# One DFF tile per weight piece: reordering how float64 weights are loaded and split in an attention and two-MLP kernel

## The chip, the cores and the metric

The kernel runs on one core of one Trainium2 chip. The metric is the device time of one execution in microseconds, the median over several runs. Engines are called as the profile calls them: PE (TensorE matmuls) and PEld (its weight loads), DVE (VectorE), ACT (ScalarE), POOL (GpSimd) and SP (SyncE, which here only issues DMAs).

## The reference

A causal attention (4 batches, 8 heads, 576 positions, head size 64; half the heads see a local window of 32, the others every 32nd position) is followed by two MLPs over 2304 tokens, each `512 -> 2048 -> 512`:

```python
scores = np.where(masks[None], scale * np.matmul(q, k.transpose(0, 1, 3, 2)), -1e9)
attn = np.exp(scores - np.max(scores, axis=-1, keepdims=True))
attn = attn / (np.sum(attn, axis=-1, keepdims=True) + 1e-09)
x = np.matmul(attn, v)            # to (2304, 512)
h = np.maximum(x @ w_in, 0.0)     # w_in  512 x 2048, float64
x = (h * h) @ w_out               # w_out 2048 x 512, float64; twice, with other weights
```

## The kernel before

**Numbers in two parts.** A matmul operand is held as a rounded part (`hi`, float32r) and a remainder (`lo`). Each product of the MLPs is three matmuls: hi by hi, hi by lo, lo by hi. The weights arrive as float64 words and are taken apart on chip, piece by piece. A piece is 128 partitions by 512 float64 (512 KB), and there are 32 in each layer. Four functions, each one step of a piece's way, are laid out in the list `conv` so that consecutive entries belong to four consecutive pieces: `sign_and_end` (two DVE instructions, L212 and L215), `exponent_range` (ACT, L221), `together` (DVE, L226), `in_parts` (ACT writes hi, L239; DVE writes lo, L240). Call the DVE part of them S, T and P. `conv_by(1)` emits the next entry of the list, wherever the program stands.

**Pieces before.** Groups of eight: four "in" pieces, each holding 128 of the 512 rows of `w_in` for 1024 words (four DFF tiles of 128 columns), then four "out" pieces, each 128 rows of `w_out`.

**Steps.** The MLP runs in 144 steps `s`, one for each token block and DFF tile: 16 steps a block of 512 tokens (8 steps, with two tiles each, for a block of 256), five blocks a layer. Layer 1 is steps 0 to 71, layer 2 steps 72 to 143. `mm1(s)` makes 12 matmuls into `ps_h` (L677); then ACT applies the ReLU (`r`, L689) and squares it into `gh` (L692), DVE squares again into `sq` (L693) and subtracts to get the remainder `gl` (L694). `mm2(s)` makes 12 matmuls into `ps_y` (L728). The program, and so each engine's queue, goes `mm1(s+1)`, `mm2(s)`, `mm1(s+2)`, `mm2(s+1)`. Each step has eight places called `point()`: three inside `mm1`, one behind it (behind r, gh, sq, gl), three inside `mm2`, one behind it. At a point, entries of the attention lists are emitted, and then one `conv` entry while the layer's pieces last.

**Attention.** Twelve fills of the first batch run alone ahead of the MLP, in the rounds of `ALONE`. After each round `START_LOAD` tells how many pieces are loaded and `START_CONV` how many conv entries are emitted. The fills of the second batch (`SHARED`) run at the points of steps 0 to 15, those of the others later. One fill has on PE scores (L417), transposes (L460), values (L476) and a last transpose (L522), on DVE a mask with maximum (L437, four pairs), a division (L507, L508, L510) and a remainder (L564).

**Between the layers.** At the end of the steps with `f % 4 == 3` of layer 1's last block (steps 59, 63, 67, 71), eight pieces of layer 2 are loaded into the slots that the old pieces leave; conv entries run at every point from step 62 on.

**Order.** No scheduler reorders anything: each engine runs its instructions in the order in which the program emits them, and all loads go through SP's queue.

Of the kernel before, what the change touches and what calls it, by code (L numbers as in the profile page):

```python
# [12 lines left out]
AF = mybir.ActivationFunctionType  # L13
ALU = mybir.AluOpType
AX = mybir.AxisListType

P = 128
# [5 lines left out]
KC = DM // P  # L23
NF = DFF // P
# [6 lines left out]
NB = len(BLOCKS[0])  # L31
# [10 lines left out]

N_PT = 8

START_LOAD = (0, 0, 0, 1, 2, 2, 4, 2, 2, 4, 2, 5, 4, 2, 2)
START_CONV = (3, 0, 0, 0, 0, 0, 0, 4, 8, 4, 2, 1, 3, 3, 6)
GAP = 80

FIRST_2 = 2
# [88 lines left out]
def r32(ap):  # L138
    return ap.bitcast(F32)
# [3 lines left out]
def tile_attention_then_two_mlps(  # L143
# [9 lines left out]
    nc = tc.nc  # L153
# [19 lines left out]
    wt = {}  # L173
    pieces = []
    for layer in range(2):
        for g in range(4):
            pieces += [("in", layer, g, c) for c in range(KC)]
            pieces += [("out", layer, g, c) for c in range(4)]
    half1 = len(pieces) // 2
    n_load = [0]  # L180
    raw, val = {}, {}

    def load_piece():

        n = n_load[0]
        if n >= len(pieces):
            return
        kind, layer, g, c = pieces[n]
        raw[n] = wpool.tile([P, 512, 2], I32, tag=f"w{n % half1}", name="raw")
        n_load[0] += 1  # L190
        if kind == "in":
            src = w_in[layer][c * P:(c + 1) * P, g * 1024:(g + 1) * 1024]
        else:
            src = w_out[layer][(4 * g + c) * P:(4 * g + c + 1) * P, :]
        nc.sync.dma_start(out=raw[n].rearrange("p n w -> p (n w)"), in_=src)

    def load_ahead(n):

# [49 lines left out]
    n_conv, n_part = [0], [0]  # L248

    def conv_by(n):  # L250

        while n and n_conv[0] < len(conv):
            fn, i = conv[n_conv[0]]
            if i >= n_load[0]:
                return
            fn(i)
            n_conv[0] += 1
            n -= 1
            n_part[0] += fn is in_parts

    def ready(key):
        while key not in wt:
            conv_by(1)
        return wt[key]
# [105 lines left out]
    def load_v():  # L370
        i = n_vin[0]
        if i >= NFILL:
            return
        n_vin[0] += 1
        _, v = src_of(i)
        vin[i] = fpool.tile([P, VW], F32, tag="v", name="v", bufs=5)
        nc.sync.dma_start(out=vin[i][:, :v.shape[-1]], in_=v)
# [115 lines left out]
    def one_small():  # L493
        if small:
            small.pop(0)()
# [130 lines left out]
    blocks = [(layer, j) for layer in range(2) for j in range(NB)]  # L626

    def tiles_of(k):
        layer, j = blocks[k]
        return TB // BLOCKS[layer][j][1]  # L630
# [23 lines left out]
    def block_x(k):  # L654
        layer, j = blocks[k]
        return (xh[j], xl[j]) if layer == 0 else xin[k]

    def mm1(s, point):

        if s >= len(steps):  # L660
            return
        k, f = steps[s]
        ne = tiles_of(k)
        n = TB // ne
        x_hi, x_lo = block_x(k)
        g, f0 = divmod(f, 4)
        if n_att[0] < len(att):
            ps = ps_h.tile([P, TB], F32, tag="h", name="ps_h")
        else:
            ps = ps_a.tile([P, TB], F32, tag="a", name="ps_h")  # L670
        for c in range(KC):
            w = ready(("in", blocks[k][0], g, c))
            for e in range(ne):
                cols = slice((f0 + e) * P, (f0 + e + 1) * P)
                for i, (a, x) in enumerate(((0, x_hi), (0, x_lo), (1, x_hi))):

                    nc.tensor.matmul(  # L677
                        ps[:, e * n:(e + 1) * n],
                        lhsT=w[:, a, cols],
                        rhs=x[:, c, :n],  # L680
                        start=c == 0 and e == 0 and i == 0,
                        stop=c == KC - 1 and i == 2 and e == ne - 1,
                    )
                    one_small()
            if c < KC - 1:
                point()
        r = gpool.tile([P, TB], F32, tag="r", name="r", bufs=1)
        sq = gpool.tile([P, TB], F32, tag="sq", name="sq", bufs=1)
        nc.scalar.activation(out=r, in_=ps, func=AF.Relu, scale=W_BACK)  # L689
        h = gpool.tile([P, TB], F32R, tag="gh", name="gh", bufs=2)  # L690
        lo = gpool.tile([P, TB], F32R, tag="gl", name="gl", bufs=2)
        nc.scalar.activation(out=h, in_=r, func=AF.Square)  # L692
        nc.vector.tensor_tensor(out=sq, in0=r, in1=r, op=ALU.mult)  # L693
        nc.vector.tensor_tensor(out=lo, in0=sq, in1=r32(h), op=ALU.subtract)  # L694
        gh[s], gl[s] = h, lo

    def mm2(s, point):
        k, f = steps[s]
        layer, j = blocks[k]
        t0, n = BLOCKS[layer][j]  # L700
        ne = tiles_of(k)
        g, f0 = divmod(f, 4)
        ws = [ready(("out", layer, g, f0 + e)) for e in range(ne)]
        h, lo = gh.pop(s), gl.pop(s)

        ny = KC if layer == 0 else n // P
        if f == 0:
            ys[k] = [ps_y.tile([P, 512], F32, tag=f"y{c}", name="ps_y") for c in range(ny)]
        end = f + ne == NF
        todo = []  # L710
        for c, y in enumerate(ys[k]):
            cols = slice(c * P, (c + 1) * P)
            for i, (a, gp) in enumerate(((0, h), (1, h), (0, lo))):
                for e, w in enumerate(ws):
                    g0 = e * n
                    rows = slice(g0 + c * P, g0 + (c + 1) * P)
                    if layer == 1:
                        todo.append((i, c, y, gp[:, rows], w[:, a]))
                    else:
                        todo.append((i, c, y[:, :n], w[:, a, cols], gp[:, g0:g0 + n]))  # L720
        if not end:

            todo.sort(key=lambda t: t[0] == 2)
        places = [-(-len(todo) * (i + 1) // 4) - 1 for i in range(3)]
        last = {t[1]: m for m, t in enumerate(todo)}
        seen = set()
        for m, (i, c, y, lhsT, rhs) in enumerate(todo):
            nc.tensor.matmul(  # L728
                y, lhsT=lhsT, rhs=rhs, start=f == 0 and c not in seen, stop=end and m == last[c]
            )  # L730
            seen.add(c)
            one_small()
            if end and m == last[c]:
                t = apool.tile([P, 512], F32, tag="pt", name="o")
                if layer == 0:
                    t = t[:, :n]
                nc.scalar.activation(out=t, in_=y, func=AF.Copy, scale=W_BACK)  # L737
                if layer == 0:
                    nc.sync.dma_start(out=y_dram[:, c, t0:t0 + n], in_=t)
                else:  # L740
                    nc.sync.dma_start(out=out[t0 + c * P:t0 + (c + 1) * P, :], in_=t)
            if m in places:
                point()
# [13 lines left out]
    with tc.manual_schedule():  # L757
        nc.scalar.dma_start(out=cst, in_=consts)
        for n in range(5):
            if n < 3:  # L760
                load_qk()
            load_v()
        rounds = 0
        while n_att[0] < att_end[0]:
            att_to(min(n_att[0] + len(ALONE), att_end[0]))
            load_ahead(START_LOAD[rounds])
            conv_by(START_CONV[rounds])
            rounds += 1
        def nothing():
            pass  # L770

        mm1(0, nothing)
        for s in range(len(steps)):
            k, f = steps[s]
            layer, j = blocks[k]
            n_pt = [0]
            load_ahead(4)
            for fn, k2, c in y_at.get(s, ()):
                fn(k2, c)

            def point(s=s, layer=layer, j=j, f=f):
                n_pt[0] += 1
                at = N_PT * s + n_pt[0]
                for b, (p0, p1) in enumerate(spans):
                    if at > p0:
                        lo, hi = att_end[b], att_end[b + 1]
                        att_to(min(hi, lo + -(-(hi - lo) * (at - p0) // (p1 - p0))))
                if n_part[0] < half1 or layer == 1 or j == NB - 1 and f > 5:
                    conv_by(1)

            mm1(s + 1, point)
            point()
            mm2(s, point)
            point()
            if layer == 0 and j == NB - 1 and f % 4 == 3:
                for _ in range(8):
                    load_piece()

# [35 lines left out]
```

## Time and profile before

| | |
|---|---|
| median of 3 runs | 923.03 us (920.58 to 923.31) |
| profiled execution, its own time | 921.91 us |
| its span | 920.1 us |
| PE / PEld busy | 898.3 / 754.5 us |
| DVE / ACT busy | 483.0 / 389.6 us |
| HBM read / written | 61.67 / 9.44 MB |

The span is what the profiler saw of the program from its first to its last instruction; the execution's own time is 1.8 us longer. Busy time of PE counts a matmul from its start to a modelled end, so that matmuls overlap.

### The profile page before, as it was taken

The numbers are of one execution on the slowest core, as the hardware profiler recorded it, in microseconds if no ns is written. First come the engines' busy times: TensorE is split into PE (matmuls) and PEld (weight loads), VectorE is DVE, ScalarE is ACT, GpSimd is POOL, SyncE is SP. The second block draws the span as 40 slices with busy tenths as digits, with TensorE's granted clock in tenths as the row PEclk, the third lists the DMA queues.
The fourth block names the chain that finished last, engine by engine and source line by source line (L and its number), as shares of the span: only waits on it lengthen the run. The fifth ranks groups of instructions, "written<-read, shape, count | busy, mean of one in ns | idle before, by whom it ended". The sixth has DMA issues, their size and how long they took to land.

```text
span 920.1 us, 12461 instructions
## 1 busy us (share of the span) xinstructions
PE 898.3 (98%) x4624; PEld 754.5 (82%) x4624; DVE 483.0 (52%) x1234; ACT 389.6 (42%) x825; POOL 0.2 (0%) x4
## 2 busy tenths in 40 slices
PE   7799999999999999999999999999999999999998
PEld 6778888877788888899887677888888888888897
DVE  5999995576666665222289996222322233222221
ACT  5656773555555544322256664232223232322222
POOL 0000000000000000000000000000000000000000
PEclk9599999999999999999999999999999999999999
DMA  8856520222222110100555140010001000100010
GB/s 271 287 171 218 191 89 13 84 79 69 87 68 101 54 61 12 46 1 24 206 194 194 61 191 12 12 69 1 23 1 69 1 24 0 58 6 7 1 46 24
DMA packets 31597, 71.92 MB, mean 78 GB/s; under 512 B 3504, under 2 KB 11824, under 8 KB 31536
## 3 DMA queue, kind: packets, MB, share of 16 engines
q1 hardware_dynamic: 31392, 70.86, 22.5%
q8 instruction: 37, 0.61, 0.3%
q10 hardware_dynamic: 144, 0.26, 0.1%
q14 instruction: 24, 0.20, 0.1%
HBM read 61.67 MB, written 9.44 MB: 77 GB/s over the span
## 4 chain that ended last, share of the span: by engine, by line
PE 86%; DVE 9%; DMA 2%; ACT 2%; issue 1%; DVEq 0%; ACTq 0%
PE ps_h L677 39%; PE ps_y L728 38%; PE ps_o L476 3%; PE ps_s L417 2%; DVE val L226 2%; DMA qk<-st_qk_d 2%; DVE w L240 2%; DVE raw L215 2%; PE ps_pt L460 2%; DVE gl L694 1%; PE ps_s L323 1%; ACT raw L221 1%; DVE raw L212 1%; PE ps_x L522 1%; ACT r L689 1%
## 5 line engine op out<-in xcount | busy, mean ns | idle before, releaser
L677 PE MATMUL ps_h<-xh,w 128*128 128x512 f32 (+1 forms) x1280 | 404.3, 376 | 4.4 <-ACT r L689 4.4
L693 DVE TENSOR_TENSOR sq<-r 128x512 f32<-128x512 f32 x144 | 99.5, 691 | 360.3 <-ACT r L689 360.0
L677 PEld LDWEIGHTS ps_h<-xh,w 128*128 128x128 f32 x1280 | 234.4, 190 | 46.8 <-ACT r L689 8.2
L689 ACT ACTIVATE r<-ps_h 128x512 f32<-128x512 f32 x144 | 86.0, 597 | 379.5 <-PE ps_h L677 349.7
L677 PE MATMUL ps_h<-xl,w 128*128 128x512 f32 (+1 forms) x640 | 237.4, 371 | 0.0
L728 PE MATMUL ps_y<-gh,w 128*128 128x512 f32 (+1 forms) x640 | 155.6, 375 | 0.0
L728 PE MATMUL ps_y<-w,gh 128*128 128x512 f32 x576 | 145.0, 390 | 0.0
L677 PEld LDWEIGHTS ps_h<-xl,w 128*128 128x128 f32 x640 | 121.4, 190 | 16.7
L728 PEld LDWEIGHTS ps_y<-w,gh 128*128 128x128 f32 x576 | 107.5, 188 | 22.6 <-ACT o L737 0.7
L728 PEld LDWEIGHTS ps_y<-gh,w 128*128 128x128 f32 x640 | 108.2, 189 | 16.7
L694 DVE TENSOR_TENSOR gl<-sq,gh 128x512 fp32r<-128x512 f32 x144 | 99.7, 693 | 17.9
L692 ACT ACTIVATE gh<-r 128x512 fp32r<-128x512 f32 x144 | 91.2, 633 | 4.6
L728 PE MATMUL ps_y<-gl,w 128*128 128x512 f32 (+1 forms) x320 | 85.2, 375 | 0.8 <-DVE gl L694 0.8
L728 PE MATMUL ps_y<-w,gl 128*128 128x512 f32 x288 | 79.1, 389 | 0.0
L728 PEld LDWEIGHTS ps_y<-gl,w 128*128 128x128 f32 x320 | 55.0, 189 | 10.7 <-DVE gl L694 1.9
L728 PEld LDWEIGHTS ps_y<-w,gl 128*128 128x128 f32 x288 | 54.1, 188 | 11.2
L453 ACT ACTIVATE s<-s,m 96x128 f32<-96x128 f32 (+2 forms) x176 | 55.9, 389 | 4.9 <-DVE m L437 4.3
L221 ACT ACTIVATE raw<-raw 128x512 f32<-128x512 f32 x64 | 43.0, 675 | 20.3 <-DVE raw L215 20.0
L239 ACT ACTIVATE w<-val 128x512 fp32r<-128x512 f32 x64 | 40.2, 629 | 22.5 <-DVE val L226 22.5
L476 PEld LDWEIGHTS ps_o<-v,pt 128*96 128x96 f32 (+2 forms) x352 | 45.2, 183 | 5.0
L215 DVE SCALAR_TENSOR_TENSOR raw<-raw 128x512 int32<-128x512 int32 x64 | 44.4, 694 | 2.2
L476 PE MATMUL ps_o<-v,pt 128*96 128x65 f32 (+2 forms) x352 | 44.4, 261 | 0.0
(34 smaller groups left out, 543.3 us busy)
## 6 DMA issues: line engine op xcount, KB each, us to landing
raw<-moe_w_in_d SPq DMA_DIRECT2D x32, 512.0 KB, 5.3
raw<-moe_w_out_d SPq DMA_DIRECT2D x32, 512.0 KB, 7.1
qk<-loc_qk_d SPq DMA_DIRECT2D x12, 416.0 KB, 3.1
out_d<-o SPq DMA_DIRECT2D x18, 256.0 KB, 2.0
y_dram<-o SPq DMA_DIRECT2D x16, 256.0 KB, 2.0
y_in<-y_dram SPq DMA_DIRECT2D x16, 256.0 KB, 2.9
qk<-loc_qk_d SPq DMA_DIRECT2D x12, 304.0 KB, 3.4
v<-loc_v_d SPq DMA_DIRECT2D x24, 130.0 KB, 2.9
```

Of the source, the lines that this page charges most:

```text
L215: nc.vector.scalar_tensor_tensor(out=lower, in0=upper, scalar=-(2 ** 31), in1=lower, op0=ALU.bitwise_and, op1=ALU.bitwise_or)
L221: nc.scalar.activation(out=upper, in_=upper, func=AF.Copy, scale=2.0 ** (W_EXP // 8 - 112))
L226: nc.vector.scalar_tensor_tensor(out=val[n].bitcast(I32), in0=upper, scalar=3, in1=lower, op0=ALU.logical_shift_left, op1=ALU.bitwise_or,)
L239: nc.scalar.activation(out=w[:, 0], in_=v, func=AF.Copy)
L453: nc.scalar.activation(out=blk, in_=blk, func=AF.Exp, scale=-1.0, bias=m[:nq, j:j + 1])
L476: nc.tensor.matmul(ps[:nq, j * W:(j + 1) * W], lhsT=pt[:nk, j * nq:(j + 1) * nq], rhs=t[:nk, j * W:(j + 1) * W], start=True, stop=True,)
L677: nc.tensor.matmul(ps[:, e * n:(e + 1) * n], lhsT=w[:, a, cols], rhs=x[:, c, :n], start=c == 0 and e == 0 and i == 0, stop=c == KC - 1 and ...
L689: nc.scalar.activation(out=r, in_=ps, func=AF.Relu, scale=W_BACK)
L692: nc.scalar.activation(out=h, in_=r, func=AF.Square)
L693: nc.vector.tensor_tensor(out=sq, in0=r, in1=r, op=ALU.mult)
L694: nc.vector.tensor_tensor(out=lo, in0=sq, in1=r32(h), op=ALU.subtract)
L728: nc.tensor.matmul(y, lhsT=lhsT, rhs=rhs, start=f == 0 and c not in seen, stop=end and m == last[c])
```

## The change

A piece of `w_in` holds all 512 rows for one DFF tile, as four runs of 1 KB in each partition where it had one run of 4 KB. Pieces alternate: "in" of tile 0, "out" of tile 0, "in" of tile 1, and so on; a step of a 512-token block needs one of each. The tables for the time of the first batch are new: 31 conv entries before, 19 now; loads are later too. Between the layers two pieces are loaded at the end of each step of the last block (56 to 71), and conv entries run from step 59 at three of four points. While loaded pieces wait to be taken apart, ACT makes `sq` (Square) and then `gh` (Copy of `sq`), and DVE only `gl`. In code:

```diff
-START_LOAD = (0, 0, 0, 1, 2, 2, 4, 2, 2, 4, 2, 5, 4, 2, 2)
-START_CONV = (3, 0, 0, 0, 0, 0, 0, 4, 8, 4, 2, 1, 3, 3, 6)
+START_LOAD = (0, 0, 0, 1, 0, 1, 0, 1, 0, 1, 1, 1, 1, 2, 2)
+START_CONV = (0, 0, 0, 0, 0, 0, 0, 0, 0, 2, 3, 3, 3, 4, 4)
...
-        for g in range(4):
-            pieces += [("in", layer, g, c) for c in range(KC)]
-            pieces += [("out", layer, g, c) for c in range(4)]
+        for f in range(NF):
+            pieces += [("in", layer, f), ("out", layer, f)]
...
+            dst = dst.rearrange("p (c m) -> p c m", c=KC)
+            src = w_in[layer].rearrange("(c p) m -> p c m", p=P)[:, :, 2 * f * P:2 * (f + 1) * P]
...
         for c in range(KC):
-            w = ready(("in", blocks[k][0], g, c))
             for e in range(ne):
+                w = ready(("in", blocks[k][0], f + e))
...
-        nc.scalar.activation(out=h, in_=r, func=AF.Square)
-        nc.vector.tensor_tensor(out=sq, in0=r, in1=r, op=ALU.mult)
+        if 0 < n_load[0] - n_part[0]:
+
+            nc.scalar.activation(out=sq, in_=r, func=AF.Square)
+            nc.scalar.activation(out=h, in_=sq, func=AF.Copy)
+        else:
+            nc.scalar.activation(out=h, in_=r, func=AF.Square)
+            nc.vector.tensor_tensor(out=sq, in0=r, in1=r, op=ALU.mult)
...
-                if n_part[0] < half1 or layer == 1 or j == NB - 1 and f > 5:
+                if n_part[0] < half1 or (layer == 1 or j == NB - 1 and f > 2) and n_pt[0] % 4:
                     conv_by(1)
...
-            if layer == 0 and j == NB - 1 and f % 4 == 3:
-                for _ in range(8):
+            if layer == 0 and j == NB - 1:
+                for _ in range(2):
                     load_piece()
```

PE's order is the same in both kernels but for which weights a matmul reads. The order in the queues is shown at two places; names carry buffer numbers where these tell pieces apart.

Place one, step 4 of layer 1. DVE before, around the remainder `gl_1009` of `mm1(4)`; `w_1033` is an "out" piece that PE first reads in `mm2(5)`:

```order
L693 TENSOR_TENSOR sq_1006<-r_1005 128x512
L694 TENSOR_TENSOR gl_1009<-sq_1006,gh_1008 128x512
L212 TENSOR_SCALAR raw_870<-raw_870 128x512
L215 SCALAR_TENSOR_TENSOR raw_870<-raw_870 128x512
L226 SCALAR_TENSOR_TENSOR val_1027<-raw_781 128x512
L240 TENSOR_TENSOR w_1033<-val_983,w_1033 128x512
L564 TENSOR_TENSOR xl_304<-ps_x_1024,xh_303 128x192
```

DVE of the change at the same place, around `gl_979` of `mm1(4)`; `w_1003` is the "in" piece of tile 5:

```order
L241 TENSOR_TENSOR w_969<-val_903,w_969 128x512
L698 TENSOR_TENSOR gl_979<-sq_976,gh_978 128x512
L213 TENSOR_SCALAR raw_840<-raw_840 128x512
L216 SCALAR_TENSOR_TENSOR raw_840<-raw_840 128x512
L227 SCALAR_TENSOR_TENSOR val_997<-raw_751 128x512
L241 TENSOR_TENSOR w_1003<-val_953,w_1003 128x512
L565 TENSOR_TENSOR xl_300<-ps_x_994,xh_299 128x192
```

The square has left DVE; S, T and P behind `gl` stand as before, but the P there now makes the weights of the next `mm1`. PE of the change from the last matmul of `mm1(4)` (`ps_h_927`) over the second half of `mm2(3)` to the start of `mm1(5)` (`ps_h_1021`), with what a matmul waits for:

```order
L676 MATMUL ps_h_927<-xh_212,w_909 128x512
L731 MATMUL ps_y_726<-gh_884,w_875 128x512 x2
L731 MATMUL ps_y_723<-gl_885,w_875 128x512
L731 MATMUL ps_y_724<-gl_885,w_875 128x512
L731 MATMUL ps_y_725<-gl_885,w_875 128x512
L731 MATMUL ps_y_726<-gl_885,w_875 128x512
L676 MATMUL ps_h_1021<-xh_212,w_1003 128x512 [waits Activation_49]
L477 MATMUL ps_o_1014<-v_553,pt_988 96x65 [waits DMAHW3_49,DVE_49]
L676 MATMUL ps_h_1021<-xl_213,w_1003 128x512
L477 MATMUL ps_o_1014<-v_553,pt_988 96x65
L676 MATMUL ps_h_1021<-xh_212,w_1003 128x512 [waits DVE_49]
```

The third matmul of `mm1(5)`, the first that reads the lo part of `w_1003`, now has a wait for DVE; in the kernel before, `mm1(5)` has none.

Place two, between the layers. DVE before, from one `gl` to the next (steps 67 and 68):

```order
L694 TENSOR_TENSOR gl<-sq,gh 128x512
L226 SCALAR_TENSOR_TENSOR val<-raw 128x512
L240 TENSOR_TENSOR w<-val,w 128x512
L212 TENSOR_SCALAR raw<-raw 128x512
L215 SCALAR_TENSOR_TENSOR raw<-raw 128x512
L650 TENSOR_TENSOR xl_4860<-y_in,xh_4859 128x512
L226 SCALAR_TENSOR_TENSOR val<-raw 128x512
L240 TENSOR_TENSOR w<-val,w 128x512
L212 TENSOR_SCALAR raw<-raw 128x512
L215 SCALAR_TENSOR_TENSOR raw<-raw 128x512
L693 TENSOR_TENSOR sq<-r 128x512
L694 TENSOR_TENSOR gl<-sq,gh 128x512
```

DVE of the change at the same steps:

```order
L698 TENSOR_TENSOR gl<-sq,gh 128x512
L241 TENSOR_TENSOR w<-val,w 128x512
L213 TENSOR_SCALAR raw<-raw 128x512
L216 SCALAR_TENSOR_TENSOR raw<-raw 128x512
L651 TENSOR_TENSOR xl_4870<-y_in,xh_4869 128x512
L227 SCALAR_TENSOR_TENSOR val<-raw 128x512
L241 TENSOR_TENSOR w<-val,w 128x512
L213 TENSOR_SCALAR raw<-raw 128x512
L216 SCALAR_TENSOR_TENSOR raw<-raw 128x512
L698 TENSOR_TENSOR gl<-sq,gh 128x512
```

One T and the square are gone from this step; other steps lose more, since six conv entries, not eight, stand in a step.

## Rows read from the trace of the kernel before

**Rows 1.** Windows: us; busy PE, PEld, DVE, ACT, POOL; PEclk, DMA share, GB/s.

```profile
22.00:45.00 23.00, 17.30 (x91) 15.63 (x91) 20.81 (x77) 15.46 (x45) 0.00 (x0) 0.57 0.86 297
55.00:156.00 101.00, 101.00 (x571) 84.74 (x570) 90.35 (x255) 65.13 (x153) 0.00 (x0) 1.00 0.41 135
482.00:568.00 86.00, 81.48 (x345) 63.46 (x344) 80.78 (x140) 52.59 (x90) 0.00 (x0) 1.00 0.33 123
568.00:920.00 352.00, 348.50 (x1628) 292.12 (x1626) 96.21 (x143) 94.49 (x160) 0.00 (x0) 1.00 0.07 22
```

**Rows 2.** Waits of PE, 0 to 46 us: total, times, longest.

```profile
PE ps_s L417 <- DMA qk<-st_qk_d: 4.5, 3, 2.4
PE ps_x L522 <- DVE xn L510: 1.8, 3, 0.9
```

**Rows 3.** Timeline of PE at the start of mm1(0): start, duration, what.

```profile
45.14 0.78 PE L677 MATMUL ps_h<-xh,w 128*128 128x512 f32 x1
```

**Rows 4.** Timeline of ACT: r of steps 1, 15, 66 and 80.

```profile
54.66 0.60 ACT L689 ACTIVATE r<-ps_h 128x512 f32<-128x512 f32 x1 [2.29 <-PE ps_h L677]
...
155.92 0.60 ACT L689 ACTIVATE r<-ps_h 128x512 f32<-128x512 f32 x1 [1.14 <-issue]
...
482.68 0.60 ACT L689 ACTIVATE r<-ps_h 128x512 f32<-128x512 f32 x1
...
566.99 0.60 ACT L689 ACTIVATE r<-ps_h 128x512 f32<-128x512 f32 x1 [2.79 <-PE ps_h L677]
```

**Rows 5.** Timeline of all engines, mm1(5)'s end to mm1(6)'s end.

```profile
84.07 0.60 ACT L689 ACTIVATE r<-ps_h 128x512 f32<-128x512 f32 x1 [2.20 <-PE ps_pt L460]
84.70 0.63 ACT L692 ACTIVATE gh<-r 128x512 fp32r<-128x512 f32 x1
...
85.50 0.69 DVE L694 TENSOR_TENSOR gl<-sq,gh 128x512 fp32r<-128x512 f32 x1
...
86.10 0.28 DVE L437 CUSTOM_DVE_ANT_0 s<-ps_s,cst 96x128 f32<-96x128 f32 x1
...
86.91 0.19 PEld L677 LDWEIGHTS ps_h<-xh,w 128*128 128x128 f32 x1
86.95 0.08 DVE L437 DVE_READ_ACCUMULATOR2_ANT m<- 96x1 f32 x1
86.95 0.42 DVE L212 TENSOR_SCALAR raw<-raw 128x512 int32<-128x512 int32 x1
87.14 0.40 PE L677 MATMUL ps_h<-xh,w 128*128 128x512 f32 x1
...
87.91 0.48 PE L677 MATMUL ps_h<-xh,w 128*128 128x512 f32 x1
...
88.01 0.68 DVE L226 SCALAR_TENSOR_TENSOR val<-raw 128x512 int32<-128x512 int32 x1
...
88.61 0.68 DVE L240 TENSOR_TENSOR w<-val,w 128x512 fp32r<-128x512 f32 x1
...
91.79 0.60 ACT L689 ACTIVATE r<-ps_h 128x512 f32<-128x512 f32 x1 [2.03 <-PE ps_pt L460]
```

**Rows 6.** Timeline: the third matmul of mm1(7), then its r.

```profile
95.33 0.62 PE L677 MATMUL ps_h<-xh,w 128*128 128x512 f32 x2
...
98.67 0.60 ACT L689 ACTIVATE r<-ps_h 128x512 f32<-128x512 f32 x1 [1.47 <-PE ps_h L677]
```

**Rows 7.** The chain that ended last: start, us, what.

```profile
45.46 4.55 PE ps_h L677 x12
...
158.58 2.72 PE ps_h L677 x12
```

**Rows 8.** DMA issues: KB each, median us from issue to landing.

```profile
raw<-moe_w_in_d SPq DMA_DIRECT2D x32, 512.0 KB, 5.3
v<-loc_v_d SPq DMA_DIRECT2D x24, 130.0 KB, 2.9
```

**Rows 9.** Windows of two microseconds, columns as in rows 1.

```profile
556.00:558.00 2.00, 0.50 (x3) 0.08 (x1) 1.97 (x5) 0.97 (x3) 0.00 (x0) 1.00 0.00 0
```

More of the change, by code (lines that the diff above doesn't have):

```diff
@@ L187, in load_piece @@
             return
-        kind, layer, g, c = pieces[n]
+        kind, layer, f = pieces[n]
         raw[n] = wpool.tile([P, 512, 2], I32, tag=f"w{n % half1}", name="raw")
         n_load[0] += 1
+        dst = raw[n].rearrange("p n w -> p (n w)")
         if kind == "in":
-            src = w_in[layer][c * P:(c + 1) * P, g * 1024:(g + 1) * 1024]
-        else:
-            src = w_out[layer][(4 * g + c) * P:(4 * g + c + 1) * P, :]
-        nc.sync.dma_start(out=raw[n].rearrange("p n w -> p (n w)"), in_=src)
+            dst = dst.rearrange("p (c m) -> p c m", c=KC)
+            src = w_in[layer].rearrange("(c p) m -> p c m", p=P)[:, :, 2 * f * P:2 * (f + 1) * P]
+        else:
+            src = w_out[layer][f * P:(f + 1) * P, :]
+        nc.sync.dma_start(out=dst, in_=src)
     def load_ahead(n):
@@ L665, in mm1 @@
         x_hi, x_lo = block_x(k)
-        g, f0 = divmod(f, 4)
         if n_att[0] < len(att):
@@ L671, in mm1 @@
         for c in range(KC):
-            w = ready(("in", blocks[k][0], g, c))
             for e in range(ne):
-                cols = slice((f0 + e) * P, (f0 + e + 1) * P)
+                w = ready(("in", blocks[k][0], f + e))
                 for i, (a, x) in enumerate(((0, x_hi), (0, x_lo), (1, x_hi))):
@@ L678, in mm1 @@
                         ps[:, e * n:(e + 1) * n],
-                        lhsT=w[:, a, cols],
+                        lhsT=w[:, a, c * P:(c + 1) * P],
                         rhs=x[:, c, :n],
@@ L701, in mm2 @@
         ne = tiles_of(k)
-        g, f0 = divmod(f, 4)
-        ws = [ready(("out", layer, g, f0 + e)) for e in range(ne)]
+        ws = [ready(("out", layer, f + e)) for e in range(ne)]
         h, lo = gh.pop(s), gl.pop(s)
```

## Prediction

> **What bounds the kernel now.** I read the windows by stage first. From 55 to 156 us, the steps with the second batch's attention and the splitting of layer 1's weights, PE has no idle time at the full granted clock, and DVE works 90.35 of 101 us [rows 1]. A busy PE need not be a PE at its peak, so I looked for its waits in that stretch: there is none. PE's own work sets the pace there, and DVE comes close behind. From 568 us on PE alone is the bound. Two stretches are different. In 22 to 45 us PE is busy for 17.30 of 23 us at a mean clock of 0.57, DVE for 20.81, and the DMA engines for 0.86 of the time [rows 1]; PE waits 4.5 us for attention's loads, which lie in the queue behind weight pieces, and 1.8 us for DVE's divisions [rows 2]. In 482 to 568 us, between the layers, DVE is busy for 80.78 of 86 us and PE's weight load row has fallen to 63.46 [rows 1]: DVE is the bound there. So two places have something to give, about 20 us of idle or slow PE, and one, steps 1 to 15, has nothing to give but can lose.
>
> **Term 1, ahead of the MLP.** The first MLP matmul stands behind the last division of the first batch on DVE. Ahead of that division, DVE's queue held 7 S, 5 T and 4 P before, and holds 5, 2 and 1 now (counted in the two queues). From start to start S takes 1.06 us (86.95 to 88.01), T 0.60 and P 0.60 [rows 5]. That is 7 x 1.06 + 9 x 0.60 = 12.8 us before and 5 x 1.06 + 3 x 0.60 = 7.1 now. DVE is nearly without gaps there [rows 1], so I take the difference, 5.7 us, and mm1(0) starts near 39.4 us instead of 45.14 [rows 3]. The loads that made PE wait meet fewer weight pieces in the queue, so that wait goes; what is late next is DVE, which is in the sum already. Low bound 4 us: the waits for divisions, 1.8 us [rows 2], are latency and stay. High bound 7.5: mm1(0) ran at half clock (the 1.2 GHz level), 4.55 us for twelve matmuls against 2.72 later [rows 7]; without the wait for loads the clock may stay up, which gives 1.8 more.
>
> **Term 2, steps 1 to 15.** This is where I expect the loss. Before, a step drew on four "in" pieces, of which only the last was finished close to its use. Now one piece holds all that `mm1(s+1)` needs, and the 19 entries emitted ahead of step 0, with eight a step from there on, put its P into the seventh point of step s-1. That is behind `gl` of `mm1(s)` in DVE's queue, as the change's rows for `w_1003` show. `gl` cannot run before `mm1(s)` has ended. So a ring closes: end of mm1(s), r, sq, gh, gl, then S, T, P on DVE, then the third matmul of mm1(s+1). `mm2(s-1)` lies in PE's queue between the two mm1, and is the only cover.
>
> The ring's length from the start of r(s), by rows 5: r to gh is 0.63 us (84.07 to 84.70). The new order has three such links in a row, r to sq, sq to gh, and gh to gl, so gl starts at 1.89 (before: 85.50 - 84.07 = 1.43). gl takes 0.60 until the next instruction (85.50 to 86.10), S 1.06, T 0.60, and P ends 0.68 after its start: 1.89 + 0.60 + 1.06 + 0.60 + 0.68 = 4.83. Where a mask or a division stands in between, 0.85 more (86.10 to 86.95): 5.68. A weight load then takes 0.23 from its start to its matmul (86.91 to 87.14), with 0.04 for the semaphore, an estimate: 0.27. In the trace of before, the third matmul of mm1(6) started 3.84 us after r(5) (87.91); by the ring it would start at 5.95. So the cover ends about 2 us too early.
>
> From the third matmul to the next r it is 3.88 us in mm1(6) (87.91 to 91.79, scores inside) [rows 5] and 3.34 in mm1(7) (95.33 to 98.67, scores behind it) [rows 6]. By the queues, mm1(2) to mm1(6) are like the first, mm1(7) to mm1(14) like the second. The fourteen intervals from r(1) to r(15):
> - four without a mask, 4.83 + 0.27 + 3.88 = 8.98 each: 35.9
> - one with a mask, 5.68 + 0.27 + 3.88: 9.8
> - six with a full mask or a division, 5.68 + 0.27 + 3.34 = 9.29 each: 55.7
> - two with half a mask, 5.26 + 0.27 + 3.34 = 8.87 each: 17.7
> - the last, with a division and P but no S and T, and ten matmuls behind the third (9 x 0.227 from rows 7, and 0.5 to r): 1.89 + 0.60 + 0.85 + 0.68 + 0.27 + 2.6 = 6.9
>
> They sum to 126.0 us. The trace has 155.92 - 54.66 = 101.3 [rows 4]. Loss: 24.7 us. Step 0 is not in it: the P of mm1(1)'s piece is emitted ahead of gl(0).
>
> Bounds: if the weight load can run early, 0.23 less in each of 14, a loss of 21.5. If one instruction of 0.60 stands ahead of gl in half of the steps, 4 more: 29. Nothing else fits into the longer step badly: DVE has 2 x 2.26 (S, T, P twice), 0.60 for gl and about 1.9 of attention, 7 us in 9; ACT loses slack to the extra 0.63, yet the hi part that PE needs follows gh by less than the DVE chain takes.
>
> **Term 3, between the layers.** From r(66) to r(80) it took 566.99 - 482.68 = 84.3 us [rows 4] where fourteen steps of 2 x 2.72 [rows 7] take 76.2. Before, a step gave DVE two pieces (4.52), sq and gl (1.20), and in some steps a remainder of y (0.60): 5.7 to 6.3, over the 5.44 of PE. Now it is one and a half pieces (3.39), gl, and the same remainder: 4.0 to 4.6. The pieces are finished many steps ahead of their use, since splitting starts 13 steps before layer 2 at 1.5 pieces a step against one "in" and one "out" used in each; no ring closes. PE is the bound again, and I take back all of 8.1 us; low bound 5, if the first steps of layer 2 still catch on something.
>
> **Edits at no cost.** An "in" piece now goes in runs of 1 KB. Attention's v has runs of 1040 B, and 130 KB of it land in 2.9 us; 512 KB in 4 KB runs land in 5.3 [rows 8]. The price of a piece is thus between 5.3 and 4 x 2.9 = 11.6 us; I take 6, as in flight they overlap. The cover is that a piece is asked for more than one step, 9 us, ahead of its S. Without it each S, and with it the ring, would be late by the difference. SP's extra issues wait only for slots between the layers; behind them stand y's loads, which have three steps until their use. ACT's Square and Copy instead of one Square add 0.63 in about 40 steps, in the ring in term 2, and covered by PE between the layers.
>
> **Sum.** The profiled execution took 921.9 us, 1.1 below the median. 921.9 - 5.7 + 24.7 - 8.1 = 932.8, and against the median 934. The bounds give 923 - 7.5 + 21.5 - 8.2 = 929 to 923 - 4 + 29 - 5 = 943. A difference of 0.3%, 2.8 us, is about what a measurement of this kernel can tell from no change.
>
> **Rivals.**
> *The ring is covered, faster.* If P came before PE asks for it, steps 1 to 15 would keep their time, and terms 1 and 3 alone give 923 - 13.8 = 909 us. For it speaks that PE waits nowhere there now, and that DVE has more room. It decides at 3.84 us behind r: P must end some 2 us earlier than the rows give. Against it is the queue order, which no engine can pass.
> The Trainium skill goes further that way: "Perfetto Trace Analysis", in "Identifying the Most-Contended Engine", tells to find the engine with the highest occupancy and optimize that first. By occupancy that is DVE in this stretch, and taking 15 squares of 0.60 from it would give 9 us more, about 900 us. The trace does not bear this out: DVE's 89% made PE wait nowhere. Together I give 0.12.
> *The ring is half covered.* If some entries of P run ahead, or PE has more work between than I count, the loss is some 12 us and the gains cancel it: about 921 us. 0.06.
> *The ring costs the clock too, much slower.* After PE had stood 2.4 us for a load [rows 2], the granted clock fell, and its mean over 22 to 45 us is 0.57 [rows 1]. With a wait of nearly 2 us in each step it could fall again and again: each mm1 at half clock costs 1.8 us [rows 7], 25 us over fourteen steps, 959 us. Against it: at 556 to 558 us PE was busy for 0.50 of 2 us and the clock stayed at 1.00 [rows 9].
> The Trainium skill has this as a rule: "TensorE: Matmul & The Clock Gate", in "HAM oscillation — how this bites in real kernels", shows a kernel whose repeated waits send the clock to half before each piece of work. By it the sum would go toward the 959. The two rows point in different directions, so it gets 0.04.
>
> **Chances.** The forecast, term 2 in full, has 0.78. Slower by over 0.3%: 0.78 less 0.02, and 0.04: 0.80. Faster: 0.12 and half of the half-covered case, 0.15. Same: 0.05. The forecast's own range is 929 to 943; to hold eight in ten I take in the half-covered case and some of the tails, 915 to 944.
>
> **What would show it.** Right: r(1) near 49 us; the waits of PE name the hi or lo part of `w` (the P line) ahead of `ps_h`, some 1.5 to 2 us in each of steps 1 to 14, with steps of about 9 us; r(15) near 175 instead of 156; from r(66) to r(80) 76 us. Wrong: steps of 7.3 us with no wait of PE for `w`, or waits that end with ACT or a DMA; a granted clock under 1 in steps 2 to 15; steps between the layers that stay over 5.6 us.

## The result, and the profile after

The changed kernel takes 935.0 us (median of 4 runs, 935.0 to 935.2) against 922.7 us for the kernel before in the same measurement (920.6 to 923.3). The ratio is 1.0138, with a 95% interval of 1.0121 to 1.0156: the change makes the kernel slower by 12 us. The prediction was 934.0 us. The profiled execution took 935.01 us, and its span is 933.1 us, 13.0 more than before's 920.1.

The stages tell three different stories. The first fence is section 1 of the page of the changed kernel, the second shows its windows (columns as in rows 1: length, then busy time of PE, PEld, DVE, ACT and POOL, granted clock, DMA share, GB/s).

```profile
PE 899.3 (96%) x4624; PEld 753.7 (81%) x4624; DVE 459.8 (49%) x1196; ACT 410.8 (44%) x863; POOL 0.2 (0%) x4
```

```profile
22.00:45.00 23.00, 17.50 (x101) 14.78 (x100) 20.61 (x79) 14.27 (x45) 0.00 (x0) 0.70 0.93 302
55.00:156.00 101.00, 88.05 (x478) 69.70 (x476) 73.61 (x222) 62.03 (x139) 0.00 (x0) 0.98 0.42 139
482.00:568.00 86.00, 86.00 (x381) 71.23 (x380) 66.12 (x116) 59.98 (x104) 0.00 (x0) 1.00 0.48 162
568.00:920.00 352.00, 352.00 (x1633) 294.90 (x1632) 106.87 (x162) 103.58 (x175) 0.00 (x0) 1.00 0.06 22
```

Over the whole program DVE lost 23 us of work and ACT gained 21, which is what the moved squares should do, and PE's work is the same (899.3 against 898.3). The time went elsewhere. In 55 to 156 us PE had no idle time [rows 1] and now has 13 us; in the same 101 us it gets through 478 matmul records where it had 571. In 482 to 568 us it is the other way round: PE was busy for 81.48 us and now has no idle time, with DVE down from 80.78 to 66.12.

The ReLU of steps 1, 15, 66 and 80 answers to rows 4. This is ACT's timeline: start, duration, instruction, and in brackets the idle time ahead of it with what ended that.

```profile
49.38 0.60 ACT L688 ACTIVATE r<-ps_h 128x512 f32<-128x512 f32 x1 [1.58 <-PE ps_h L676]
...
177.04 0.60 ACT L688 ACTIVATE r<-ps_h 128x512 f32<-128x512 f32 x1 [1.07 <-PE ps_h L676]
...
503.75 0.60 ACT L688 ACTIVATE r<-ps_h 128x512 f32<-128x512 f32 x1 [1.39 <-PE ps_h L676]
...
579.91 0.60 ACT L688 ACTIVATE r<-ps_h 128x512 f32<-128x512 f32 x1 [0.39 <-PE ps_h L676]
```

From the start to r(1): 49.4 us where it was 54.7, 5.3 less. From r(1) to r(15): 127.7 where it was 101.3, 26.4 more. From r(15) to r(66): 326.7, as before (326.8). From r(66) to r(80): 76.2 where it was 84.3, 8.15 less. From there to step 143's r: 344.2, as before (344.1). The sum, -5.3 + 26.4 - 8.15 = +12.95, is the 13.0 by which the span grew.

The windows above hold other steps in the change than in the kernel before, since its steps begin at other times. The same columns from r(1) to r(15) and from r(66) to r(80) of the change:

```profile
49.38:177.04 127.66, 109.93 (x571) 86.25 (x570) 88.96 (x254) 76.76 (x172) 0.00 (x0) 0.97 0.37 121
503.75:579.91 76.16, 76.16 (x337) 63.08 (x336) 58.47 (x102) 53.16 (x93) 0.00 (x0) 1.00 0.35 122
```

So of the 26.4 us that steps 1 to 15 lost, PE was idle for 17.7. For the other 8.7 it shows as busy, with as many matmul records as before (571). Between the layers it has no idle time left.

PE's waits over the whole run (total, times, longest) say what it stood idle for:

```profile
PE ps_h L676 <- DVE w L241: 13.2, 12, 1.9
...
PE ps_h L676 <- ACT w L240: 4.2, 5, 1.5
PE ps_x L523 <- DVE xn L511: 3.0, 4, 2.0
PE ps_x L523 <- DMA raw<-moe_w_out_d: 2.2, 1, 2.2
```

The two rows on `ps_h` are new and lie in steps 1 to 15: `mm1` waits 17.4 us in all for the two halves of a weight piece, the lo part from DVE (P, L241) and the hi part from ACT (L240). In steps 1 and 2 it waits for hi alone, from step 6 on for lo alone. The waits for `st_qk`, 4.5 us before [rows 2], are gone. One step, read from the timeline of all engines, shows how such a wait comes about:

```profile
85.46 0.60 ACT L688 ACTIVATE r<-ps_h 128x512 f32<-128x512 f32 x1 [2.99 <-PE ps_h L676]
86.09 0.63 ACT L693 ACTIVATE sq<-r 128x512 f32<-128x512 f32 x1
86.76 0.63 ACT L694 ACTIVATE gh<-sq 128x512 fp32r<-128x512 f32 x1
87.42 0.69 DVE L698 TENSOR_TENSOR gl<-sq,gh 128x512 fp32r<-128x512 f32 x1 [2.60 <-ACT gh L694]
...
88.49 0.63 ACT L240 ACTIVATE w<-val 128x512 fp32r<-128x512 f32 x1
...
88.87 0.42 DVE L213 TENSOR_SCALAR raw<-raw 128x512 int32<-128x512 int32 x1
89.17 0.50 PE L676 MATMUL ps_h<-xh,w 128*128 128x512 f32 x1 [0.42 <-ACT w L240]
...
89.94 0.68 DVE L227 SCALAR_TENSOR_TENSOR val<-raw 128x512 int32<-128x512 int32 x1
90.54 0.68 DVE L241 TENSOR_TENSOR w<-val,w 128x512 fp32r<-128x512 f32 x1
91.27 0.19 PEld L676 LDWEIGHTS ps_h<-xh,w 128*128 128x128 f32 x1 [1.17 <-DVE w L241]
91.28 0.50 PE L676 MATMUL ps_h<-xh,w 128*128 128x512 f32 x1 [1.03 <-DVE w L241]
```

Read it as a ring: PE's end of `mm1(s)` lets ACT make r, sq, gh; gh ends DVE's idle time of 2.60 us; behind `gl` in DVE's queue stand S, T and P; and P ends PE's wait of 1.03 us in `mm1(s+1)`. DVE, the engine that PE waits for, is itself idle for 2.6 us of this step.

### The profile page after: what moved, and what is told of

It is laid out like the page before. It is cut to its first block, busy times and chain, and to the rows that moved or that the text cites. A ratio compares the mean times of both kernels' runs of the same rounds, so it can differ in the third digit from the quotient of the medians.

```text
span 933.1 us, 12404 instructions
## 1 busy us (share of the span) xinstructions
PE 899.3 (96%) x4624; PEld 753.7 (81%) x4624; DVE 459.8 (49%) x1196; ACT 410.8 (44%) x863; POOL 0.2 (0%) x4
## 4 chain that ended last, share of the span: by engine, by line
PE 88%; DVE 6%; ACT 4%; issue 1%; DMA 1%; SPq 0%; DVEq 0%; ACTq 0%
PE ps_h L676 43%; PE ps_y L731 37%; PE ps_o L477 3%; PE ps_s L418 2%; PE ps_pt L461 1%; ACT r L688 1%; PE ps_s L324 1%; DVE gl L698 1%; ACT sq L693 1%; DVE raw L216 1%; DVE w L241 1%; ACT gh L694 1%; PE ps_x L523 1%; DVE val L227 1%; DVE s L438 1%
## 5 line engine op out<-in xcount | busy, mean ns | idle before, releaser
L697 DVE TENSOR_TENSOR sq<-r 128x512 f32<-128x512 f32 x106 | 73.3, 692 | 328.5 <-ACT r L688 328.2
L696 ACT ACTIVATE gh<-r 128x512 fp32r<-128x512 f32 x106 | 67.2, 634 | 3.4
L241 DVE TENSOR_TENSOR w<-val,w 128x512 fp32r<-128x512 f32 x64 | 43.7, 684 | 4.1 <-ACT w L240 4.0
```

What stands on the lines that cost most here:

```text
L241: nc.vector.tensor_tensor(out=w[:, 1], in0=v, in1=r32(w[:, 0]), op=ALU.subtract)
```

## The experiments

The theory: DVE's queue order closes this ring, because the P that `mm1(s+1)` needs stands behind `gl` of `mm1(s)`. If so, a few entries emitted ahead of step 0 are enough to open it. Rival A: the extra pass on ACT is what costs the time, since it makes `gh`, and all that ACT has behind it, later. Rival B: the "in" pieces, now in runs of 1 KB, land late. Neither would mind four entries emitted earlier.

In each run r(1), r(15), r(66) and r(80) are read as above. The kernel before had medians of 922.8, 922.8 and 922.2 us in the three measurements (e1 to e4, e5 to e7, e8).

| kernel | r(1) | r(1) to r(15) | r(66) to r(80) | median, us | ratio to before, 95% interval |
|---|---|---|---|---|---|
| before | 54.7 | 101.3 | 84.3 | 922.7 | |
| the change | 49.4 | 127.7 | 76.2 | 935.0 | 1.0138 (1.0121 to 1.0156) |
| e1_gl_later | 48.0 | 109.3 | 76.2 | 917.3 | 0.9945 (0.9925 to 0.9965) |
| e2_four_more | 48.0 | 101.6 | 76.2 | 908.8 | 0.9858 (0.9831 to 0.9885) |
| e3_squares_dve | 49.0 | 117.8 | 76.2 | 925.8 | 1.0034 (1.0019 to 1.0049) |
| e4_turn_only | 54.8 | 101.2 | 76.2 | 913.5 | 0.9902 (0.9878 to 0.9926) |
| e5_old_tables | 52.8 | 101.6 | 76.2 | 915.5 | 0.9929 (0.9906 to 0.9952) |
| e6_later_front | 49.0 | 101.6 | 76.2 | 908.2 | 0.9850 (0.9829 to 0.9871) |
| e7_gl_later_sq_dve | 48.8 | 108.7 | 76.2 | 916.1 | 0.9935 (0.9914 to 0.9956) |
| e8_last_rounds_free | 50.8 | 101.6 | 76.2 | 910.2 | 0.9871 (0.9850 to 0.9892) |

**e2: four entries more ahead of step 0.** The change with 23 entries instead of 19:

```diff
-START_CONV = (0, 0, 0, 0, 0, 0, 0, 0, 0, 2, 3, 3, 3, 4, 4)
+START_CONV = (0, 0, 0, 0, 0, 0, 0, 0, 0, 2, 3, 3, 3, 4, 8)
```

> The change, with one number: eight conv entries, not four, in the last round ahead of the MLP, so that every P stands four entries earlier, ahead of gl. Ring theory: intervals r(1) to r(15) fall to 101 to 104 us; one more S, T, P ahead of step 0 costs up to 2.3 us; total 908 to 913 us. Rivals A and B: ACT's and the DMAs' work is the same, total near 935 (B: or later still, since S asks for each piece four entries earlier).

It took 908.8 us. Steps 1 to 15 take 101.6 us, and between 48 and 170 us PE waits nowhere. The same step from the timeline of all engines:

```profile
85.45 0.60 ACT L688 ACTIVATE r<-ps_h 128x512 f32<-128x512 f32 x1 [1.81 <-PE ps_h L676]
86.13 0.68 DVE L241 TENSOR_TENSOR w<-val,w 128x512 fp32r<-128x512 f32 x1
...
87.41 0.69 DVE L698 TENSOR_TENSOR gl<-sq,gh 128x512 fp32r<-128x512 f32 x1 [0.59 <-ACT gh L694]
...
88.58 0.40 PE L676 MATMUL ps_h<-xh,w 128*128 128x512 f32 x1
...
89.04 0.63 PE L676 MATMUL ps_h<-xh,w 128*128 128x512 f32 x2
```

The P that `mm1(6)` needs now runs at 86.13, in the time in which DVE had waited for `gh`, and `gl` comes behind it at 87.41, as late as in the change. ACT makes the same extra pass, and the pieces are the same: with four entries moved, all 26 us of the loss are gone. So Rivals A and B fall as causes of their own, and the ring as the cause is shown. Against Rival B speaks also that in the change nothing waits for a piece to land: the five rows of DVE's own waits from 40 to 180 us name ACT or PE, none a DMA.

**e1: the same tables, but `gl` steps out of P's way.** While pieces are being taken apart, `gl` of a step is emitted behind the three points of `mm2`, so that S, T and P no longer stand behind it:

```diff
+    late = []
...
-        nc.vector.tensor_tensor(out=lo, in0=sq, in1=r32(h), op=ALU.subtract)
+        def rest():
+            nc.vector.tensor_tensor(out=lo, in0=sq, in1=r32(h), op=ALU.subtract)
+        if 0 < n_load[0] - n_part[0] and s > 0:
+            late.append(rest)
+        else:
+            rest()
...
             mm2(s, point)
+            while late:
+                late.pop()()
```

> The change, with one edit: while pieces wait, the remainder gl of a step stands behind the step's last P in DVE's queue (after the three points of mm2), not ahead of S, T and P. Ring theory: P no longer waits for the mm1 before it, so the 14 intervals from r(1) to r(15), 127.6 us in the change, fall to 101 to 108 (some waits for the hi part on ACT, which still stands behind r, sq and gh), and the total to 909 to 916 us. Rival A (ACT's second pass for gh is what costs): ACT has the same work, so the intervals stay near 127 and the total near 935. Rival B (pieces in runs of 1 KB land late): no change either, 935.

It took 917.3 us, and steps 1 to 15 take 109.3, a little over what was expected. No wait for DVE is left; PE's waits from 48 to 170 us are one row:

```profile
PE ps_h L678 <- ACT w L240: 4.3, 6, 1.5
```

What is late next is the hi part, on ACT. In the step at 83 us, from ACT's timeline:

```profile
83.03 0.60 ACT L690 ACTIVATE r<-ps_h 128x512 f32<-128x512 f32 x1 [2.52 <-PE ps_h L678]
...
86.07 0.62 ACT L240 ACTIVATE w<-val 128x512 fp32r<-128x512 f32 x1
```

Between r and hi stand sq, gh and three passes of other work, and hi ends 3.66 us after r began: a second ring, over ACT's queue. What the extra pass has to do with it, e7 asks. The change has this ring too. These are the first matmuls of `mm1(2)` and `mm1(3)` there:

```profile
53.61 0.50 PE L676 MATMUL ps_h<-xh,w 128*128 128x512 f32 x1 [1.55 <-ACT w L240]
...
62.83 0.50 PE L676 MATMUL ps_h<-xh,w 128*128 128x512 f32 x1 [0.83 <-ACT w L240]
```

In these two steps no wait for DVE is named, and they last as long with DVE's ring open: from r(1) to r(2) 8.85 us in the change and 8.79 in e1, from r(2) to r(3) 9.19 and 9.20.

**e3: all squares back on DVE**, the pieces and tables as in the change:

```diff
-        if 0 < n_load[0] - n_part[0]:
+        if False:
```

> The change without its third part: ACT squares into gh and DVE into sq at all times, as before. Ring theory: r to gl falls from 1.96 to about 1.43 us in the ring, 0.5 us in each of 14 intervals: r(1) to r(15) 119 to 122 us; between the layers DVE has 0.6 us more in a step, 4.6 to 5.2, still under PE's 5.44: 76 to 77 us for r(66) to r(80); total 927 to 931 us. Rival A: the whole loss of 26 us goes, total near 909. If instead DVE's load is what matters, steps get slower and the total passes 938.

It took 925.8 us, 9 us less than the change, and steps 1 to 15 take 117.8, both a little under what was expected. PE's waits from 48 to 178 us, and then the window between the layers:

```profile
PE ps_h L676 <- DVE w L241: 9.4, 12, 1.6
PE ps_h L676 <- ACT w L240: 1.8, 3, 0.9
```

```profile
482.00:568.00 86.00, 86.00 (x381) 71.19 (x381) 76.51 (x132) 49.74 (x89) 0.00 (x0) 1.00 0.40 138
```

DVE does more and PE waits less. Between the layers PE stays without idle time with the squares on DVE, which is then busy for 76.51 of 86 us: 1.5 pieces a step suffice there.

**e4: the kernel before, with the new rate and ACT's squares between the layers alone.** Old pieces, old tables, and:

```diff
-        nc.scalar.activation(out=h, in_=r, func=AF.Square)
-        nc.vector.tensor_tensor(out=sq, in0=r, in1=r, op=ALU.mult)
+        if half1 <= n_part[0] < n_load[0]:
+            nc.scalar.activation(out=sq, in_=r, func=AF.Square)
+            nc.scalar.activation(out=h, in_=sq, func=AF.Copy)
+        else:
+            nc.scalar.activation(out=h, in_=r, func=AF.Square)
+            nc.vector.tensor_tensor(out=sq, in0=r, in1=r, op=ALU.mult)
...
-                if n_part[0] < half1 or layer == 1 or j == NB - 1 and f > 5:
+                if n_part[0] < half1 or (layer == 1 or j == NB - 1 and f > 5) and n_pt[0] % 4:
```

> The kernel before, with nothing but the part between the layers: conv entries at three of four points there (from step 62 on) and the squares on ACT while layer 2's pieces wait; pieces, loads and tables as before. By term 3 r(66) to r(80) falls from 84.3 to 76 or 77 us and the total by 8 us, to 914 to 916; the rest of the kernel stays within 1 us. Rival: the gain between the layers comes from loading two pieces a step rather than eight at once, and without it the total stays within 3 us of 923.

It took 913.5 us. Everything up to r(66) is as before, and the turn takes 76.2 us, as in the change. So the gain of term 3 does not need the new pieces, nor two loads a step: e4 loads eight at once, as before, and the rival falls. And e3 does without ACT's squares there. What the two share with the change is the rate, three points of four. It was not tried alone, so that it suffices is not shown.

**e5: the change with the tables of before.**

```diff
-START_LOAD = (0, 0, 0, 1, 0, 1, 0, 1, 0, 1, 1, 1, 1, 2, 2)
-START_CONV = (0, 0, 0, 0, 0, 0, 0, 0, 0, 2, 3, 3, 3, 4, 4)
+START_LOAD = (0, 0, 0, 1, 2, 2, 4, 2, 2, 4, 2, 5, 4, 2, 2)
+START_CONV = (3, 0, 0, 0, 0, 0, 0, 4, 8, 4, 2, 1, 3, 3, 6)
```

> The change with the two tables of the kernel before (31 conv entries and many early loads ahead of step 0), all else as in the change. This takes term 1 alone back. By term 1, r(1) comes again at 54 to 55 us (48.0 to 49.4 with the new tables); by the ring theory the twelve entries more keep P ahead of gl, so r(1) to r(15) is 101 to 103 us; between the layers 76 us. Total 908.8 (the run with four more entries) plus 6.7: 914 to 917. A theory in which the new piece form, and not the entries of the tables, brings the early start gives r(1) near 49 and a total near 909.

It took 915.5 us. With 31 entries ahead of step 0 no ring closes (101.6 us), and r(1) comes at 52.8. PE's wait for attention's loads ahead of the MLP is back:

```profile
PE ps_s L418 <- DMA qk<-st_qk_d: 5.6, 3, 2.5
```

The profiled execution of e5 took 912.3 us, 3.1 below its median, so its r(1) of 52.8 (54 to 55 were expected) is early. By the medians e5 is 6.6 us above e2, and the two agree from r(1) on; by the profiled executions r(1) is 4.8 us later. Either way most or all of the gain in front belongs to the tables, not to the form of the pieces.

**e6 and e8: where the front's limit lies.** e6 spreads 23 entries so that fewer stand ahead of the last divisions, e8 leaves two of the last rounds free:

```diff
-START_CONV = (0, 0, 0, 0, 0, 0, 0, 0, 0, 2, 3, 3, 3, 4, 4)
+START_CONV = (0, 0, 0, 0, 0, 0, 0, 0, 0, 1, 2, 2, 4, 2, 12)    # e6
+START_CONV = (0, 0, 0, 0, 0, 0, 0, 0, 0, 2, 3, 5, 0, 0, 13)    # e8
```

> The change with 23 conv entries ahead of step 0 as in the run with four more, but placed later: 1, 2, 2, 4, 2, 12 in the last six rounds. Ahead of the last division of the first batch stand 4 S and 2 T (5.4 us), not 5 S, 2 T and 1 P (7.1). By term 1 r(1) comes 1 to 2 us earlier than 48.0, at 46 to 47; r(1) to r(15) stays at 101 to 103. Total 905 to 908 us, and 2 us less again if PE's waits there grow so short that the clock stays up. If the waits for divisions are latency and not DVE's queue, r(1) stays at 48 and the total at 909.

> The change with 23 conv entries ahead of step 0, placed 2, 3, 5, 0, 0, 13 in the last six rounds: no entry between the last two divisions of the first batch, where PE waited 1.98 us in the two runs before. The reading to test: not the sum of the entries ahead of the last division sets the start of mm1(0), but those that stand directly between one division and the next, where PE has nothing else. Then PE's wait of 1.98 us falls under 0.6, the round before it gets up to 1.2 us longer (five entries there), mm1(0) starts 0.5 to 1.5 us earlier than in the run with four more entries (39.18), and the total is 906 to 908.5. By the sum of entries (5 S, 3 T and 1 P ahead of the last division, 7.7 us, against 7.1) it would start 0.6 us later, total 909 to 910.

e6 took 908.2 us, the same as e2 within the measurement, with r(1) at 49.0; e8 took 910.2. In e8 the last wait for a division is 0.78 us instead of 1.98, but a wait for ACT stands in its place, and after a later wait of 1.90 us the granted clock falls to 0.5 from 45.3 to 48.7 us. Its PE timeline:

```profile
34.20 1.70 PE L477 MATMUL ps_o<-v,pt 108*108 108x65 f32 x8 [1.24 <-ACT pt L469]
...
38.88 0.44 PE L523 MATMUL ps_x<-cst,xn 108*128 108x108 f32 x1 [0.78 <-DVE xn L511]
...
45.24 0.80 PE L676 MATMUL ps_h<-xh,w 128*128 128x512 f32 x1 [1.90 <-ACT r L688]
```

mm1(0) starts at 39.9 us in the change, 39.2 in e2, 38.8 in e6 and 39.0 in e8. Ahead of the last division e6 has 4 S and 2 T, and e8 has 4 S, 2 T and 1 P in its trace (6.0 us, not the 7.7 of its expectation). In e1, with the 7.1 us of the change, mm1(0) starts at 38.8 as well. So 1 or 2 us of entries more or less do not show, and neither reading in e8's expectation held.

**e7: e1 and e3 together**, to see whether e1's waits for hi are due to the extra pass on ACT.

> The run with gl behind the last P, with the squares on DVE as in the kernel before. In that run PE still waited 4.3 us for the hi part, which ACT writes behind r, sq and gh; r(1) to r(15) was 109.3 us. If that is a second ring over ACT, one pass of 0.63 us less ahead of the hi part shortens it: the waits for the hi part fall under 1.5 us, r(1) to r(15) to 102 to 106 us, the total from 917 to 911 to 914. If DVE's load is what holds those steps, they get longer: over 110 us, total over 918.

It took 916.1 us, and steps 1 to 15 take 108.7 instead of the 102 to 106 expected. PE's waits from 48 to 170 us, and a step of the timeline:

```profile
PE ps_h L678 <- ACT w L240: 1.8, 3, 0.9
PE ps_h L678 <- DVE w L241: 1.5, 2, 0.8
```

```profile
89.90 0.60 ACT L690 ACTIVATE r<-ps_h 128x512 f32<-128x512 f32 x1 [2.70 <-PE ps_pt L461]
90.53 0.69 DVE L699 TENSOR_TENSOR sq<-r 128x512 f32<-128x512 f32 x1 [0.66 <-ACT r L690]
...
93.64 0.68 DVE L241 TENSOR_TENSOR w<-val,w 128x512 fp32r<-128x512 f32 x1
94.38 0.74 PE L678 MATMUL ps_h<-xh,w 128*128 128x512 f32 x2 [0.80 <-DVE w L241]
```

The waits for hi fell from 4.3 to 1.8 us (under 1.5 was expected), but the square itself waits for r and stands ahead of S, T and P, so that part of the ring over DVE closed again. The test was not clean: it does not price the extra pass alone.

## Why the prediction was right, point by point

**Term 1, ahead of the MLP: the size was right, its working is not borne out.** 5.7 us were forecast, and r(1) came 5.3 us earlier (48.0 to 49.4 in the kernels with this front). The prediction got its number by counting the DVE entries that no longer stand ahead of the last division. e6 and e8 emit fewer there than the change, and `mm1(0)` gained 1.1 us at most (r(1) at 49.0 in e6, not the 46 to 47 that counting gave), no more than e1 gained with the same entries. e5, with the old tables, brings back the entries and the wait for `st_qk` together, so it does not tell which of them cost the time. The prediction named that wait as something that goes; it then let the sum rest on DVE. That the count gave the right size may be luck. The granted clock does not explain it either: its mean over 22 to 45 us is 0.57 before [rows 1] and 0.70 in the change, but e4, whose front is that of the kernel before, has 0.73 there and starts `mm1(0)` at 45.1 all the same. What sets the start near 39 us stays open. One row misleads here: the wait of 2.2 us that the profile puts down to `raw<-moe_w_out_d` is ended by a DVE division that two S and a mask stood ahead of. In e3 and e7 the profile names the division for the same wait. DVE is busy for 1.93 us of these two (a window of the change, columns as in rows 1):

```profile
28.00:30.00 2.00, 0.36 (x4) 0.18 (x2) 1.93 (x13) 1.55 (x3) 0.00 (x0) 1.00 0.83 262
```

**Term 2, the ring: right in mechanism and nearly in size.** From the start of r to the end of P the prediction had 5.68 us with a mask between, and the step shown above has 5.76 (85.46 to 91.22). From P's end to the matmul it had 0.27, and the trace has 0.06 (91.22 to 91.28): the weight load waits for P too, but its row starts at 91.27, next to the matmul's and not 0.23 ahead of it. In size that is the lower bound, though no load ran early. The predicted steps were four of 8.98, one of 9.8, six of 9.29, two of 8.87 and one of 6.9; the trace has 8.85, 9.19, 9.21, 8.83, 11.25, 9.19, 9.18, 9.23, 8.79, 8.84, 9.35, 8.61, 10.52 and 6.62. Twelve of fourteen lie within 0.7 us of their forecast. The loss was 26.4 us instead of 24.7, and the two that stand out hold more than the difference: 11.25 is 1.4 over its 9.8, and 10.52 is 1.2 over 9.29 or 1.65 over 8.87, some 2.8 us together. They are the two steps in which the granted clock fell (below), and the ring alone comes to about 26.4 - 2.8 = 23.6. PE's idle time, 17.7 us, is less than that, since it shows as busy for 8.7 us more; the half clock is a part of these, and no view itemises the rest. One step of the working failed in a small place: "the hi part that PE needs follows gh by less than the DVE chain takes" overlooks that the first matmul needs hi, two matmuls ahead of lo. In steps 1 and 2 hi, behind r, sq, gh and other passes in ACT's queue, is what PE waits for. And PE waits 0.7 to 1.9 us in a step, mostly less than the 1.5 to 2 that the prediction gave as its sign. Five of the seventeen waits end with ACT, which the prediction has under both signs: hi as right, ACT as wrong.

**Term 3, between the layers: 8.15 us against 8.1.** PE is the bound again. The reason is narrower than the prediction's list: e4 shows that the new pieces are not needed for it, e3 that ACT's squares are not. With the slower rate (argued, not shown, since it was not tried alone) DVE's share per step falls below PE's 5.44 us either way, by the prediction's own numbers (3.39 + 1.20 + 0.60 = 5.2 with both squares on DVE).

**Edits at no cost: held.** The "in" pieces in runs of 1 KB land in 5.1 us (6 were assumed), the "out" pieces in 3.8, and neither a matmul nor a DVE instruction of steps 1 to 15 waits for a load:

```profile
raw<-moe_w_in_d SPq DMA_DIRECT2D x32, 512.0 KB, 5.1
raw<-moe_w_out_d SPq DMA_DIRECT2D x32, 512.0 KB, 3.8
```

The extra ACT pass is in the ring, as forecast, and has no price of its own between the layers (e3 and the change both take 76.2 us there).

**The rivals.** *The ring is covered, 909 us:* it is not what the change does, but it is what e2 does, and the price was right, 908.8 us. The prediction saw that P would have to end 2 us earlier; four entries make it so. That rival's further 9 us for the squares taken off DVE did not come: e5 has the squares on ACT and no ring, and its steps 1 to 15 take 101.6 us, as the 101.3 before. The Trainium skill's advice in "Perfetto Trace Analysis", "Identifying the Most-Contended Engine", is to optimize the engine with the highest occupancy first. It points to DVE here only because that page judges PE by other measures, such as the busy share of its weight loads (84.74 of 101 us, against DVE's 90.35 [rows 1]); by its busy row PE leads with 101.00. Read as taking work off DVE, the advice is not borne out in this stage. With the ring closed, relieving DVE of the squares made the ring longer by a pass of ACT, and giving them back (e3) made the kernel 9 us faster. Steps 1 to 15 gained 9.9 us; 2.8 of that are the falls of the clock, of which e3 has none there, and 7.1 are left for the ring, against 14 x (1.89 - 1.43) = 6.4 from the prediction's own lengths of r to `gl`. *The ring is half covered:* refuted, the intervals are the whole ring's. *The ring costs the clock too:* true in 2 of 14 steps, though the prediction had a granted clock under 1 in these steps among its signs of being wrong. In the change the granted clock is 0.5 (the 1.2 GHz level) from 91.6 to 95.0 us and from 166.7 to 170.1. Windows around the first fall:

```profile
89.00:91.00 2.00, 1.07 (x6) 0.79 (x6) 1.97 (x4) 2.00 (x7) 0.00 (x0) 1.00 0.51 177
...
93.00:95.00 2.00, 2.00 (x6) 1.46 (x6) 1.55 (x3) 0.00 (x0) 0.00 (x0) 0.50 0.12 33
```

PE was busy for 1.07 of two us ahead of the fall. The same repeated waits in the other twelve steps left the clock at full speed, so the cost was 2.8 us and not the 25 of that rival. "TensorE: Matmul & The Clock Gate" of the Trainium skill ("HAM oscillation — how this bites in real kernels") describes a kernel whose clock falls ahead of every piece of work; this trace has such a fall in two of fourteen steps. Why only these two steps fell is open.

**The total.** In the profiled executions the kernel lost 13.1 us (921.9 to 935.0) where the sum had 10.9: 0.4 of the difference is term 1 and 1.7 is term 2. That the medians come within 1 us of the 934.0 is partly luck.

## What to carry to other kernels

When a change gathers all that the next step needs into one late piece, follow that piece through each engine's queue and ask what it stands behind: if that is work which waits for the step before, a ring closes, and its length, not any engine's busy time, sets the pace. A ring needs little to open: four queue entries emitted ahead (e2, e6) turned 12 us of loss into 14 us of gain over the kernel before. Taking work off a busy engine by adding a pass to another can then cost time: here the ring runs through both, and with the ring open it gained nothing (e5).

## What the runs showed of the hardware

The granted clock fell to 0.5 after short waits of PE: in the change, ahead of the first of its two falls in steps 1 to 15, PE had waited 0.42 and 1.03 us (0.5 from 91.6 to 95.0 us), and in e8 once for 1.90 us (0.5 from 45.3 to 48.7 us). From the end of a DVE instruction to the start of the matmul that waited for it took only 0.06 us (91.22 to 91.28), and its weight load started 0.05 us after that end.
